# Attention mix on one core: the clamp pass writes the first exponential slice itself, and part of the last fold moves ahead of the last B unit

## The chip, the core and the metric

The kernel runs on one core of one Trainium2 chip. The metric is device microseconds of one execution.

Names of the engines: PE is the matrix engine (PEld its weight loads), VectorE is "DVE" in the profile, ScalarE is "ACT", GpSimd is "POOL", SP issues most DMAs.

## The reference

Two attention blocks on the same input, gated per token:

```python
def reference(A_x, A_wqkv, A_wo, B_x, B_wqkv, B_wo, gate_w):
    x = A_x                                   # [1, 2048, 640]
    g = _sigmoid((x * gate_w).sum(-1, keepdims=True))
    a = _A_ref(x, A_wqkv, A_wo)               # 32 heads of 20, full softmax attention over 2048 keys
    b = _B_ref(x, B_wqkv, B_wo)               # 32 heads, each query sees 8 keys, 2 apart
    return g * a + (1 - g) * b
```

## The kernel before

Everything is in bf16 with fp32 sums. Block A is cut into 2048 "units": one head, 128 keys, 512 queries. Each unit needs a score matmul, 512 exponentials per partition, and a value matmul. Block B is cut into eight token units of 256 tokens; each has projections, eight product passes on VectorE, a small softmax, eight more product passes, and a summation on PE. The whole of B's work, the projections of A, and the output folds are "side work": they run in gaps.

The instruction order is made at build time by a scheduler written in the kernel file. It keeps its own estimate of each engine's clock and decides tile by tile.

**A tile and its third bank.** PSUM is used in full: two score buffers of three banks each, one bank for the value sums (`obank`), one side bank. (The Trainium skill, "PSUM — Partial Sum Buffer", section "Specifications (TRN2)", gives eight banks of 512 fp32 values per partition; 3 + 3 + 1 + 1 is eight.) A tile of scores always fills the first two banks of a score buffer, and ScalarE turns them into exponentials with one instruction. The third bank has three possible users: a third unit for ScalarE, a unit for VectorE (a "ride"), or side work.

```python
BANKS = [(sbank, 0), (score[0], 1024), (score[1], 1024)]   # side bank, third bank of each score buffer
...
def next_tile():
    x = 1 + s % 2
    free = not bank_used[x] and bank_free[x] <= now + XTOL and not crowded(x)
    n = 3 if free else 2
    ...
        if len(us) == 2 and not ride:
            ride = wanted(...)                 # give the third bank to VectorE?
            if ride:
                break
        us.append(...)                         # else a unit for ScalarE
```

**Rides.** VectorE makes exponentials from integers: a number written as the bit pattern of a bf16 is a power of two with a straight line between, and four shifted copies ("slices"), weighted and summed by the value matmul, smooth that line. Four rides of one key block make a "quad".

```python
def wanted(js):
    idle = max(now, exps[s - 2].end + LAT["act"]) + 0.4 - sch.avail["dve"]
    if idle < -DWAIT:
        return None
    if not dopen:                              # a new quad would have to be opened
        if ulock[len(dquads) % 2] or len(dquads) > cur["pv"] + 1 or now < D0 or not (
                idle >= DIDLE2 or idle >= DIDLE and done.get(...) and
                bdone[0] >= (now - BT0) / (BT1 - BT0) * BALL):
            return None                        # at most two quads open; B must be on schedule
    ...
# clamp pass, one per ride, from PSUM:
uD[d % 2][:, 512 * i:512 * (i + 1)], side[x], UOFF, 0.0, op0=ALU.add, op1=ALU.max
# slice passes, four per quad, 2048 elements:
for k in range(K):
    eD[:, sl % NS, 0:512 * n].bitcast(I16), uD[d % 2][:, 0:512 * n], 0.25, SHIFTS[k], op0=ALU.mult, op1=ALU.add
```

**Side work and third banks.** Side work normally has only the side bank. It may take third banks as well when block B is behind a straight-line schedule:

```python
XPRIO, XLATE, XT0, XT1 = 2.5, 6.6, 150.0, 880.0
def xprio():                                   # priority up to which side work may take third banks
    return XPRIO if bdone[0] >= (sch.avail["pe"] - XT0) / (XT1 - XT0) * BALL else XLATE
```

B's priority is 6, so it passes only when it is late. `bdone` sums the VectorE time that B has had; `BALL` is its total.

**The last fold.** For the last 512 tokens, partial output sums (`gen_prefold`) are made ahead of the last head group, once B is done and the other head groups are normalised.

Of the kernel before, what the change touches and what calls it, by code (L numbers as in the profile page):

```python
# [5 lines left out]
FP32 = mybir.dt.float32  # L6
# [8 lines left out]
P = 128  # L15
# [28 lines left out]
LN2 = 0.6931471805599453  # L44
STEP = 512.0
OCT = STEP * SCALE / LN2
TOP = 96
UOFF = 31 * STEP
SHIFTS = (12024.625, 12055.875, 12088.375, 12120.125)
WEIGHTS = (1.0, 0.83984375, 0.71484375, 0.59375)  # L50
K = len(SHIFTS)

# [208 lines left out]
def _build(ctx, nc, A_x, A_wqkv, A_wo, B_wqkv, B_wo, gate_w, out):  # L261
# [29 lines left out]
    ND = 2  # L291
    dst = [sb([P, 512], BF16, "dst%d" % i) for i in range(ND)]
    qbnd = sb([P, 512], BF16, "qbnd")
# [6 lines left out]

    uD = [sb([P, 4 * 512], U16, "uD%d" % i) for i in range(2)]
    gtr = uD[1][:, 0:1024].bitcast(FP32)
# [5 lines left out]
    gwT = sb([P, CN], BF16, "gwT")  # L308
    qabs = [sb([P, 512], BF16, "qabs%d" % i) for i in range(2)]
    kmx4 = sb([P, 4], FP32, "kmx4")  # L310
# [389 lines left out]
    def gen_d(d):  # L700

        n = len(ridden[d])
        while d > 0 and not done.get(("dq", d - 1)):
            yield ("cond",)
        g, kb = dquads[d]
        q = GROUPS[g][1]
        while cur["pv"] < d - 1 or not done.get(("v", kb, q // 4)):
            yield ("cond",)
        for k in range(1, K):
            T("pool", 0.3, lambda e, k=k: e.tensor_scalar(  # L710
                vS[:, d % 2, k - 1, :], _ap(vA, (kb * NQ + q) * 4 * DV, [[1, 4 * DV]]), WEIGHTS[k], None, op0=ALU.mult),
              reads=[("vA", kb, q // 4), "vAones"], writes=[("vS", d % 2, k)])
        for k in range(K):
            sl = sbase[d] + k
            while npv[0] <= sl - NS:
                yield ("cond",)
            yield ("dve", DAHEAD, sch.free(("eD", sl % NS)))
            T("dve", 0.11 + 0.1334 * n, lambda e, k=k, sl=sl: e.tensor_scalar(  # L718
                eD[:, sl % NS, 0:512 * n].bitcast(I16), uD[d % 2][:, 0:512 * n], 0.25, SHIFTS[k], op0=ALU.mult, op1=ALU.add),
              reads=[("uD", d % 2, i) for i in range(n)], writes=[("eD", sl % NS)])  # L720
            done[("ds", d, k)] = True
        ulock[d % 2] = False
        done[("dq", d)] = True

# [157 lines left out]

    pre = lambda i: stage[:, i * 1024:(i + 1) * 1024].bitcast(FP32)
    tail_bank = {}
# [9 lines left out]
    def gen_prefold():  # L894
        while not (done.get(("b", 2 * QCN - 1)) and all(done.get(("norm", POS[QCN - 1, q])) for q in range(1, NQ))):
            yield ("cond",)
        rd = [("oTd", (QCN - 1) % 2, q) for q in range(1, NQ)] + ["woA_d", "woBp"] + [
            ("oB", hu, f0) for hu in range(2) for f0 in range(0, CN, 2)]
        qs = None
        for i in range(3):  # L900
            b = yield from bank()
            if i < 2:
                yield from mm_group(b, fold_mms(side[b][:, :], 2 + i, qs, 0, 512, True), rd, mmc(512))
            else:
                for blk in range(4):
                    yield from mm_group(b, fold_mms(side[b][:, blk * P:(blk + 1) * P], blk, qs, 512, D, True), rd, mmc(128), per=3)
            yield ("dve",)
            t = T("dve", dvc(512), lambda e, b=b, i=i: e.tensor_copy(pre(i), side[b][:, :]), reads=[("side", b)],
                  writes=[("pre", i)] + [("prod", w) for w in range(5)])
            release(b, t)  # L910
        done["prefold1"] = True
# [10 lines left out]
    def gen_prefold2():  # L922
# [4 lines left out]
        qs = None  # L927
        for blk in range(2):
            b = yield from bank()
            yield from mm_group(b, fold_mms(side[b][:, :], blk, qs, 0, 512, True), rd, mmc(512), last=False)  # L930
            tail_bank[blk] = b
        done["prefold"] = True

    def tail():
# [15 lines left out]
        mm(("score", 1), [fold_mms(b3[:, blk * P:(blk + 1) * P], blk, q, 512, D, False)[0] for blk in range(4)], False)  # L950
        for blk in range(2):
            b = tail_bank[blk]
            mm(("side", b), fold_mms(side[b][:, :], blk, q, 0, 512, False), True)
        for blk in (2, 3):
            mm(("score", 0), fold_mms(score[0][:, (blk - 2) * 512:(blk - 1) * 512], blk, q, 0, 512, False), False)
        T("dve", dvc(512), lambda e: e.tensor_tensor(
            _ap(stage, 3 * 1024 + 512, [[D, 4], [1, P]]), _ap(b3, 0, [[P, 4], [1, P]]),
            stage[:, 2048:3072].bitcast(FP32).rearrange("p (b c) -> p b c", c=P), ALU.add),
          reads=[("score", 1), ("pre", 2)], writes=["tout_r"])
        for blk in range(2):  # L960
            b = tail_bank[blk]
            T("act", actc(512), lambda e, b=b, blk=blk: e.activation(tcol(blk, 0, 512), side[b][:, :], ACTF.Copy),
              reads=[("side", b)], writes=[("tout", blk)])
        for blk in (2, 3):
            T("dve", dvc(512), lambda e, blk=blk: e.tensor_tensor(
                tcol(blk, 0, 512), score[0][:, (blk - 2) * 512:(blk - 1) * 512], pre(blk - 2), ALU.add),
              reads=[("score", 0), ("pre", blk - 2)], writes=[("tout", blk)])
        for blk in range(4):
# [82 lines left out]
    XT0 = 150.0  # L1051
    XT1 = 880.0

# [191 lines left out]
    BT0 = 230.0  # L1245
    BT1 = 900.0
    BALL = 186.0
# [62 lines left out]
    def d_close():  # L1310
# [4 lines left out]
        if ridden[d]:  # L1315
            nsl[0] += K
            add_gen(gen_d(d), DLOW + 0.0001 * d)
        else:
            ulock[d % 2] = False
            done[("dq", d)] = True  # L1320
# [45 lines left out]
    def qk(s):  # L1366
# [22 lines left out]
        if rides[s]:  # L1389

            run_dve(t.end + LAT["pe"] - RFILL)
            t = T("dve", 0.69, lambda e: e.tensor_scalar(  # L1392
                uD[d % 2][:, 512 * i:512 * (i + 1)], side[x], UOFF, 0.0, op0=ALU.add, op1=ALU.max),
              reads=[("side", x)], writes=[("uD", d % 2, i)])
# [4 lines left out]
    def exp(s):  # L1399
# [5 lines left out]
        if n == 3:  # L1405
            bank_free[x] = exps[s].end + LAT["act"]

    def pv(units, slices):

# [9 lines left out]
        for d, k in slices:  # L1419
            g, kb = dquads[d]  # L1420
            sl = (sbase[d] + k) % NS
            rd.add(("eD", sl))
            if k:
                rd.add(("vS", d % 2, k))
            for i, j in enumerate(ridden[d]):
                v = vS[:, d % 2, k - 1, j * DV:(j + 1) * DV] if k else vA[:, kb, GROUPS[g][1], j, :]
                lst.append((g, kb, j, v, eD[:, sl, 512 * i:512 * (i + 1)]))
            left_d[g] -= len(ridden[d])
            npv[0] += 1
        for g, kb, j, _, _ in lst:  # L1430
# [68 lines left out]
    def pv_slot(s, force=False):  # L1499
# [10 lines left out]
        while not first and cur["pv"] < len(dquads) and dquads[cur["pv"]][0] == pvg and len(slices) < NS:  # L1510
# [9 lines left out]
            if not ok:  # L1520
                urge(d, DHIGH)
                run_until(("ds", d, k), DHIGH)
            elif not end_g and sch.ready(("eD", (sbase[d] + k) % NS)) > sch.avail["pe"]:
                break
# [9 lines left out]
    def slices_ready():  # L1534
# [4 lines left out]
        n = 0  # L1539
        while n < NS and k + n < K and done.get(("ds", d, k + n)) and sch.ready(  # L1540
                ("eD", (sbase[d] + k + n) % NS)) <= sch.avail["pe"]:
            n += 1
# [86 lines left out]
```

## Time and profile before

| | before |
|---|---|
| time, median of three runs | 881.18 us (879.49 to 881.99); with a fourth run, used from "The result" on, 880.38 us |
| units on ScalarE / rides on VectorE | 1768 / 280 |
| exponential instructions | 754: 260 of three units, 494 of two (280 with a ride, 214 without) |
| last exponential ends | 865.7 us of a span of 879.1 us |

The next line is the first part of the page: busy us of each engine, share of the span, instruction count.

```profile
PE 852.9 (97%) x13406; PEld 312.7 (36%) x13406; DVE 701.7 (80%) x1192; ACT 834.9 (95%) x788; POOL 226.7 (26%) x309
```

The groups by shape: line, engine, operation, out<-in, shapes, count | busy us, mean ns of one | idle time of the engine just before, and what ended it.

```profile
L1402 ACT ACTIVATE ebuf<-score 128x1024 bf16<-128x1024 f32 x494 | 475.4, 1037 | 15.2 <-PE score L1379 13.5 <-ACT ebuf L1402 0.2
L1402 ACT ACTIVATE ebuf<-score 128x1536 bf16<-128x1536 f32 x260 | 364.3, 1471 | 7.0 <-PE score L1379 5.9 <-ACT ebuf L1402 0.3
...
L718 DVE TENSOR_SCALAR eD<-uD 128x2048 int16<-128x2048 uint16 x280 | 190.5, 705 | 14.1 <-PE obank L1441 13.5
L1392 DVE TENSOR_SCALAR uD<-score 128x512 uint16<-128x512 f32 x280 | 187.7, 683 | 43.5 <-PE score L1379 41.6
...
L487 PE MATMUL side<-xT,kvw 128*32 128x256 bf16 x1920 | 76.3, 275 | 2.1 <-DVE qkvB L769 1.6 <-DVE oB L876 0.2 <-DVE qbnd L614 0.2
...
L487 PE MATMUL score<-xT,kvw 128*32 128x256 bf16 x480 | 19.6, 274 | 0.0
```

ScalarE's exponentials fill the run. A ride costs VectorE a clamp of 0.68 us and a quarter of four slice passes. And B's projections (the 128x256 matmuls on `xT,kvw`, 2400 in all) run to one fifth in third banks: out is `score` for 480 of them.

The end of the run, as a timeline (start us, us, engine and line, what, count, idle before):

```profile
846.29 0.42 DVE L876 SCALAR_TENSOR_TENSOR oB<-side,rB 128x256 bf16<-128x256 f32 x1 [0.52 <-PE side L487]
...
852.79 0.61 PE L487 MATMUL score<-woBp,oB 128*32 128x512 bf16 x8 [0.32 <-DMA oTd<-oN]
...
861.61 4.13 ACT L1402 ACTIVATE ebuf<-score 128x1536 bf16<-128x1536 f32 x3
874.23 0.60 ACT L962 ACTIVATE stage<-side 128x512 bf16<-128x512 f32 x1 [8.48 <-PE side L943]
```

The last exponential ends at 861.61 + 4.13 = 865.74 us, and 13.4 us of tail follow. The first leftover fold had waited for a DMA that brings normalised rows, not for B: the last B unit ends with the last write of `oB`, its output, at 846.7 us, 19 us before the last exponential ends.

A caution on PE: its 97% includes filler matmuls that keep it busy (1832 of 13406). The Trainium skill, "Perfetto Trace Analysis", section "Identifying the Most-Contended Engine", warns that matmul busy time does not say well how close PE is to its peak.

### The profile page before, as it was taken

What the parts mean: (1) busy time and instruction counts of PE and PEld (TensorE: products, weight loads), DVE (VectorE), ACT (ScalarE), POOL (GpSimd) and SP (SyncE); (2) the same over time, 40 slices, a digit from 0 to 9 for tenths busy, and PEclk for the clock granted to TensorE, in tenths of its full rate; (3) what the DMA queues carried; (4) which work ended last, traced back from release to release, by engine and by line L of the source; (5) the groups of instructions that cost most, each with busy time, mean ns of one, the idle gap of its engine ahead of it and who ended that gap; (6) DMA issues with size and microseconds to landing.
All of it is one profiled execution on the core that took longest, in us unless ns stands there. A gap on an engine that the chain in (4) does not pass through costs nothing.

```text
span 879.1 us, 31181 instructions
## 1 busy us (share of the span) xinstructions
PE 852.9 (97%) x13406; PEld 312.7 (36%) x13406; DVE 701.7 (80%) x1192; ACT 834.9 (95%) x788; POOL 226.7 (26%) x309
## 2 busy tenths in 40 slices
PE   8999999999989999999999999999999999999997
PEld 4333333434333333433333333333343334333223
DVE  6567778888788776988888997887887788989864
ACT  5999999999989999999999999999999999999994
POOL 5031027411331212152322133221023312312320
PEclk9999999999999999999999999999999999999999
DMA  9112112001010101010000100010010000100000
GB/s 292 33 39 45 43 31 71 17 15 29 23 28 23 41 21 25 13 28 20 21 18 17 34 20 20 27 28 14 13 36 20 21 19 27 27 12 12 24 6 32
DMA packets 40893, 28.19 MB, mean 32 GB/s; under 512 B 23732, under 2 KB 39556, under 8 KB 40756
## 3 DMA queue, kind: packets, MB, share of 16 engines
q1 hardware_dynamic: 40756, 26.20, 11.4%
q8 instruction: 106, 1.74, 0.8%
q14 instruction: 31, 0.25, 0.1%
HBM read 11.94 MB, written 2.62 MB: 17 GB/s over the span
## 4 chain that ended last, share of the span: by engine, by line
PE 78%; ACT 10%; DVE 6%; POOL 3%; issue 3%; DMA 0%; SPq 0%; DVEq 0%; ACTq 0%; POOLq 0%
PE score L1379 23%; PE obank L1441 18%; PE side L487 16%; ACT ebuf L1402 9%; PE score L487 8%; PE obank L1462 4%; PE score L1462 3%; PE side L1462 2%; POOL vS L710 1%; DVE eD L718 1%; PE side L798 1%; POOL kvw L732 1%; DVE stage L785 1%; POOL oN L690 1%; DVE oTt L679 0%
## 5 line engine op out<-in xcount | busy, mean ns | idle before, releaser
L1402 ACT ACTIVATE ebuf<-score 128x1024 bf16<-128x1024 f32 (+1 forms) x754 | 819.3, 1186 | 22.2 <-PE score L1379 19.5
L1379 PE MATMUL score<-qT,kT 32*128 32x512 bf16 x2048 | 298.4, 384 | 10.6 <-ACT ebuf L1402 7.5
L1392 DVE TENSOR_SCALAR uD<-score 128x512 uint16<-128x512 f32 x280 | 187.7, 683 | 43.5 <-PE score L1379 41.6
L718 DVE TENSOR_SCALAR eD<-uD 128x2048 int16<-128x2048 uint16 x280 | 190.5, 705 | 14.1 <-PE obank L1441 13.5
L710 POOL TENSOR_SCALAR vS<-vA 128x84 bf16<-128x84 bf16 x210 | 145.7, 697 | 128.3 <-PE obank L1441 118.4
L1379 PEld LDWEIGHTS score<-qT,kT 32*128 32x128 bf16 x2048 | 73.8, 91 | 269.8 <-issue 127.4
L1441 PE MATMUL obank<-ebuf,vA 128*21 128x512 bf16 x1768 | 164.0, 385 | 3.6 <-ACT ebuf L1402 1.2
L685 POOL TENSOR_TENSOR rcp<-rcp,gA 128x16 f32<-128x16 f32 x31 | 12.4, 400 | 463.1 <-DVE rcp L683 463.1
L487 PE MATMUL side<-xT,kvw 128*32 128x256 bf16 (+1 forms) x2030 | 85.6, 281 | 2.1 <-DVE qkvB L769 1.6
L1441 PE MATMUL obank<-eD,vS 128*21 128x512 bf16 x840 | 73.7, 381 | 0.0
L1441 PEld LDWEIGHTS obank<-ebuf,vA 128*21 128x21 bf16 x1768 | 40.3, 89 | 86.5 <-issue 70.7
L1462 PE MATMUL obank<-xT,zero 128*32 128x512 bf16 x808 | 66.8, 384 | 0.0
L1462 PE MATMUL score<-xT,ident 128*32 128x512 bf16 x708 | 59.2, 382 | 0.0
L487 PEld LDWEIGHTS side<-xT,kvw 128*32 128x32 bf16 x2030 | 48.0, 96 | 30.8 <-issue 16.1
L785 DVE TENSOR_TENSOR stage<-qkvB 128x1280 bf16<-128x1280 bf16 x64 | 52.9, 856 | 0.1
L861 DVE TENSOR_TENSOR stage<-qkvB,repB 128x1280 bf16<-128x1280 bf16 x64 | 50.7, 816 | 0.6 <-DMA repB<-eB 0.5
L487 PE MATMUL side<-stage,ident 128*32 128x512 bf16 (+1 forms) x704 | 44.9, 348 | 0.0
L487 PE MATMUL score<-xT,kvw 128*32 128x256 bf16 (+2 forms) x730 | 41.8, 311 | 0.0
L769 DVE CAST qkvB<-side 128x512 bf16<-128x512 f32 (+1 forms) x57 | 33.9, 595 | 7.2 <-PE side L487 7.0
L690 POOL TENSOR_TENSOR oN<-oTt,rcp 128x512 bf16<-128x512 f32 x31 | 35.1, 1131 | 2.4
L679 DVE STREAM_TRANSPOSE oTt<-obank 128x512 f32<-128x512 f32 x32 | 22.8, 713 | 9.7 <-PE obank L1441 9.1
L692 DVE STREAM_TRANSPOSE oN<-oN 128x512 bf16<-128x512 bf16 x32 | 22.4, 700 | 6.7 <-POOL oN L690 6.5
(165 smaller groups left out, 674.0 us busy)
## 6 DMA issues: line engine op xcount, KB each, us to landing
repB<-eB SPq DMA_DIRECT2D x128, 32.0 KB
WqP<-in_A_wqkv_dram SPq DMA_DIRECT2D x16, 160.0 KB
stage<-in_B_wqkv_dram SPq DMA_DIRECT2D x1, 2400.0 KB
oTd<-oN SPq DMA_DIRECT2D x108, 20.0 KB
qT<-dst SPq DMA_DIRECT2D x104, 20.0 KB
out_dram<-outsb SPq DMA_DIRECT2D x12, 160.0 KB
kvw<-in_A_wqkv_dram SPq DMA_DIRECT2D x2, 800.0 KB
oTd<-in_A_x_dram SPq DMA_DIRECT2D x2, 640.0 KB
```

Of the source, the lines that this page charges most:

```text
L487: ins = e.matmul(o[j:k, :], l[:, j:k], r, start=(first and i == 0), stop=(last and i == n - 1), skip_group_check=True)
L690: T(en, c2, lambda e: e.tensor_tensor(oo, ii, ib, ALU.mult), reads=["rcp", "oTt"], writes=["oN0"])
L710: T("pool", 0.3, lambda e, k=k: e.tensor_scalar(vS[:, d % 2, k - 1, :], _ap(vA, (kb * NQ + q) * 4 * DV, [[1, 4 * DV]]), WEIGHTS[k], None, ...
L718: T("dve", 0.11 + 0.1334 * n, lambda e, k=k, sl=sl: e.tensor_scalar(eD[:, sl % NS, 0:512 * n].bitcast(I16), uD[d % 2][:, 0:512 * n], 0.25, ...
L769: t = TB(dvc(n * TOK), lambda e, o=o, i=i: e.tensor_copy(o, i), reads=[("side", b)], writes=[key])
L785: TB(dvc(CN * TOK, 2), lambda e, w=w, ks=ks: e.tensor_tensor(prodB(w), qB[:, :, :], ks, ALU.mult), reads=["qB", "kB"], writes=[("prod", w) ...
L861: TB(dvc(CN * TOK, 2), lambda e, w=w, vs=vs, rr=rr: e.tensor_tensor(prodB(w), vs, rr, ALU.mult), reads=["vB", ("repB", w4 % 2)], writes=[( ...
L1379: ins = e.matmul(o, kT[32 * j:32 * j + 32, q, kb * P:(kb + 1) * P], qT[g % NQT][32 * j:32 * j + 32, :], start=True, stop=True)
L1392: t = T("dve", 0.69, lambda e: e.tensor_scalar(uD[d % 2][:, 512 * i:512 * (i + 1)], side[x], UOFF, 0.0, op0=ALU.add, op1=ALU.max), reads=[ ...
L1402: exps[s] = T("act", actc(512 * n), lambda e: e.activation(ebuf[s % NE][:, 0:512 * n], score[s % 2][:, 0:512 * n], ACTF.Exp, scale=LN2 / S ...
L1441: ins = e.matmul(obank[32 * j:32 * j + DV, :], v, src, start=(kb == 0), stop=(last and k >= len(lst) - 4), skip_group_check=True)
L1462: ins = e.matmul(o[32 * j:32 * j + 32, :], w[:, 32 * j:32 * j + 32] if best else w[:, :], xT[:, 0, 0:512], start=bool(best), stop=bool(bes ...
```

## The change

The intent: choose the integer step so that the clamp pass already writes the bit pattern of a bf16, that is, slice 0. Three integer additions make the other slices. VectorE saves one slice pass in four. The scheduler's constants are retuned, and the leftover folds of the first two token blocks need only the second-last B unit, so they can go ahead of the last one.

```diff
-STEP = 512.0
+STEP = 128.0
-UOFF = 31 * STEP
-SHIFTS = (12024.625, 12055.875, 12088.375, 12120.125)
-WEIGHTS = (1.0, 0.83984375, 0.71484375, 0.59375)
+SHIFTS = (0, 32, 64, 96)
+WEIGHTS = (1.0, 0.83984375, 0.70703125, 0.59375)
+UOFF = 15992.765
...
-            T("pool", 0.3, lambda e, k=k: e.tensor_scalar(
+            T("pool", 0.7, lambda e, k=k: e.tensor_scalar(
...
-        for k in range(K):
-            sl = sbase[d] + k
+        for k in range(1, K):
+            sl = sbase[d] + k - 1
...
-                eD[:, sl % NS, 0:512 * n].bitcast(I16), uD[d % 2][:, 0:512 * n], 0.25, SHIFTS[k], op0=ALU.mult, op1=ALU.add),
+                eD[:, sl % NS, 0:512 * n].bitcast(I16), uD[d % 2][:, 0:512 * n].bitcast(I16), SHIFTS[k], None, op0=ALU.add),
...
+        done[("dq", d)] = True
+        while not done.get(("p0", d)):
+            yield ("cond",)
         ulock[d % 2] = False
-        done[("dq", d)] = True
...
-        while not (done.get(("b", 2 * QCN - 1)) and all(...)):
+        while not (done.get(("b", 2 * QCN - 2)) and all(...) and done.get(("q", NG - 1))):
...
-    XT1 = 880.0
+    XT1 = 860.0
-    BT1 = 900.0
+    BT1 = 880.0
...
-                uD[d % 2][:, 512 * i:512 * (i + 1)], side[x], UOFF, 0.0, op0=ALU.add, op1=ALU.max),
+                uD[d % 2][:, 512 * i:512 * (i + 1)].bitcast(I16), side[x], UOFF, 0.0, op0=ALU.add, op1=ALU.max),
...
+                src = eD[:, sl, 512 * i:512 * (i + 1)] if k else uD[d % 2][:, 512 * i:512 * (i + 1)]
```

(The wait for `p0` holds the u-buffer until the value matmul has used slice 0. Cut: the places where partial sums are stored, the order of blocks in the tail, bookkeeping of slices. The 0.3 and 0.7 are only what the scheduler assumes for a GpSimd instruction; the instruction is the same.)

More of the change, by code (lines that the diff above doesn't have):

```diff
@@ L291, in _build @@
     ND = 2
-    dst = [sb([P, 512], BF16, "dst%d" % i) for i in range(ND)]
+    dst2 = sb([P, ND * 512], BF16, "dst")
+    dst = [dst2[:, i * 512:(i + 1) * 512] for i in range(ND)]
     qbnd = sb([P, 512], BF16, "qbnd")
@@ L299, in _build @@
     gA = [sb([P, 16], FP32, "gA%d" % i) for i in range(2)]
-    uD = [sb([P, 4 * 512], U16, "uD%d" % i) for i in range(2)]
+    uD = [sb([P, 4 * 512], BF16, "uD%d" % i) for i in range(2)]
     gtr = uD[1][:, 0:1024].bitcast(FP32)
@@ L308, in _build @@
     gwT = sb([P, CN], BF16, "gwT")
-    qabs = [sb([P, 512], BF16, "qabs%d" % i) for i in range(2)]
+    qabs2 = sb([P, 2 * 512], BF16, "qabs")
+    qabs = [qabs2[:, i * 512:(i + 1) * 512] for i in range(2)]
     kmx4 = sb([P, 4], FP32, "kmx4")
@@ L879, in gen_b @@
         done[("b", u)] = True
-    pre = lambda i: stage[:, i * 1024:(i + 1) * 1024].bitcast(FP32)
+    pre = lambda i: (dst2[:, 0:1024], qabs2[:, :], stage[:, 2048:3072])[i].bitcast(FP32)
     tail_bank = {}
@@ L894, in gen_prefold @@
     def gen_prefold():
-        while not (done.get(("b", 2 * QCN - 1)) and all(done.get(("norm", POS[QCN - 1, q])) for q in range(1, NQ))):
+        while not (done.get(("b", 2 * QCN - 2)) and all(done.get(("norm", POS[QCN - 1, q])) for q in range(1, NQ))
+                   and done.get(("q", NG - 1))):
             yield ("cond",)
-        rd = [("oTd", (QCN - 1) % 2, q) for q in range(1, NQ)] + ["woA_d", "woBp"] + [
-            ("oB", hu, f0) for hu in range(2) for f0 in range(0, CN, 2)]
         qs = None
         for i in range(3):
+            while i == 2 and not done.get(("b", 2 * QCN - 1)):
+                yield ("cond",)
+            rd = [("oTd", (QCN - 1) % 2, q) for q in range(1, NQ)] + ["woA_d", "woBp"] + [
+                ("oB", hu, f0) for hu in range(1 + (i == 2)) for f0 in range(0, CN, 2)]
             b = yield from bank()
             if i < 2:
-                yield from mm_group(b, fold_mms(side[b][:, :], 2 + i, qs, 0, 512, True), rd, mmc(512))
+                yield from mm_group(b, fold_mms(side[b][:, :], i, qs, 0, 512, True), rd, mmc(512))
             else:
@@ L908, in gen_prefold @@
             t = T("dve", dvc(512), lambda e, b=b, i=i: e.tensor_copy(pre(i), side[b][:, :]), reads=[("side", b)],
-                  writes=[("pre", i)] + [("prod", w) for w in range(5)])
+                  writes=[("pre", i)] + [[("dst", 0), ("dst", 1)], [("qabs", 0), ("qabs", 1)], [("prod", w) for w in range(5)]][i])
             release(b, t)
@@ L927, in gen_prefold2 @@
         qs = None
-        for blk in range(2):
+        for blk in (2, 3):
             b = yield from bank()
@@ L950, in tail @@
         mm(("score", 1), [fold_mms(b3[:, blk * P:(blk + 1) * P], blk, q, 512, D, False)[0] for blk in range(4)], False)
-        for blk in range(2):
+        for blk in (2, 3):
             b = tail_bank[blk]
             mm(("side", b), fold_mms(side[b][:, :], blk, q, 0, 512, False), True)
-        for blk in (2, 3):
-            mm(("score", 0), fold_mms(score[0][:, (blk - 2) * 512:(blk - 1) * 512], blk, q, 0, 512, False), False)
+        for blk in range(2):
+            mm(("score", 0), fold_mms(score[0][:, blk * 512:(blk + 1) * 512], blk, q, 0, 512, False), False)
         T("dve", dvc(512), lambda e: e.tensor_tensor(
@@ L959, in tail @@
           reads=[("score", 1), ("pre", 2)], writes=["tout_r"])
-        for blk in range(2):
+        for blk in (2, 3):
             b = tail_bank[blk]
@@ L963, in tail @@
               reads=[("side", b)], writes=[("tout", blk)])
-        for blk in (2, 3):
+        for blk in range(2):
             T("dve", dvc(512), lambda e, blk=blk: e.tensor_tensor(
-                tcol(blk, 0, 512), score[0][:, (blk - 2) * 512:(blk - 1) * 512], pre(blk - 2), ALU.add),
-              reads=[("score", 0), ("pre", blk - 2)], writes=[("tout", blk)])
+                tcol(blk, 0, 512), score[0][:, blk * 512:(blk + 1) * 512], pre(blk), ALU.add),
+              reads=[("score", 0), ("pre", blk)], writes=[("tout", blk)])
         for blk in range(4):
@@ L1315, in d_close @@
         if ridden[d]:
-            nsl[0] += K
+            nsl[0] += K - 1
+            done[("ds", d, 0)] = True
             add_gen(gen_d(d), DLOW + 0.0001 * d)
@@ L1406, in exp, with slice_keys @@
             bank_free[x] = exps[s].end + LAT["act"]
+    def slice_keys(d, k):
+        return [("eD", (sbase[d] + k - 1) % NS)] if k else [("uD", d % 2, i) for i in range(len(ridden[d]))]
     def pv(units, slices):
@@ L1420, in pv @@
             g, kb = dquads[d]
-            sl = (sbase[d] + k) % NS
-            rd.add(("eD", sl))
+            rd.update(slice_keys(d, k))
+            sl = (sbase[d] + k - 1) % NS
             if k:
                 rd.add(("vS", d % 2, k))
+                npv[0] += 1
+            else:
+                done[("p0", d)] = True
             for i, j in enumerate(ridden[d]):
                 v = vS[:, d % 2, k - 1, j * DV:(j + 1) * DV] if k else vA[:, kb, GROUPS[g][1], j, :]
-                lst.append((g, kb, j, v, eD[:, sl, 512 * i:512 * (i + 1)]))
+                src = eD[:, sl, 512 * i:512 * (i + 1)] if k else uD[d % 2][:, 512 * i:512 * (i + 1)]
+                lst.append((g, kb, j, v, src))
             left_d[g] -= len(ridden[d])
-            npv[0] += 1
         for g, kb, j, _, _ in lst:
@@ L1522, in pv_slot @@
                 run_until(("ds", d, k), DHIGH)
-            elif not end_g and sch.ready(("eD", (sbase[d] + k) % NS)) > sch.avail["pe"]:
+            elif not end_g and sch.ready(*slice_keys(d, k)) > sch.avail["pe"]:
                 break
@@ L1539, in slices_ready @@
         n = 0
-        while n < NS and k + n < K and done.get(("ds", d, k + n)) and sch.ready(
-                ("eD", (sbase[d] + k + n) % NS)) <= sch.avail["pe"]:
+        while n < NS and k + n < K and closed[d] and ridden[d] and done.get(("ds", d, k + n)) and sch.ready(
+                *slice_keys(d, k + n)) <= sch.avail["pe"]:
             n += 1
```

## The prediction

> **What bounds the kernel now.** ScalarE. The table of busy shares gives ScalarE 834.9 us of 879.1 (95%), of which 819.3 us are the 754 exponentials (costliest groups). In every 40 us stretch from 40 to 840 us it is busy 37.1 to 39.9 us; the rest is start (first exponential at 21.2 us) and tail (last one ends near 865.8 us). PE shows 97%, but 1832 of its matmuls (the groups of the filler line) are filler; in fours at about 0.22 us a set they are some 100 us (estimate), so PE has slack. VectorE shows 80%.
>
> Of 2048 score units (128x512), VectorE takes 280 ("rides", 70 quads of four), ScalarE 1768. By form, a two-unit exponential takes 1.037 us and a three-unit one 1.471 us, so a unit moved off ScalarE is worth about 0.43 us there. The schedule, made at build time, lets units ride as it sees room on VectorE; so the time follows VectorE's cost per ride.
>
> **What the change removes.** Before, a quad costs four clamp passes from PSUM (0.683 us each) and four slice passes of 2048 elements (0.705 us mean, 0.684 median). After, the clamp output is itself slice 0, and three integer adds follow. So one slice pass in four goes: 70 x 0.60 to 0.70 us = 42 to 49 us of VectorE at today's number of rides (in the timeline, passes in a row start 0.60 us apart).
>
> The remaining passes should keep their duration. The Trainium skill, "VectorE: DVE Perf Modes", section "The perf-mode tier table", puts one-source 16-bit SBUF-to-SBUF operations in the 4x mode; today's pass at 0.62 to 0.68 us for 2048 elements fits, and the add is again one-source. The clamp still reads fp32 from PSUM: 0.68 us.
>
> VectorE's 13.5 us of waits before slices, for the matmul that frees a slice buffer, should shrink.
>
> **Added or moved.** Each additional ride puts four instead of one value matmuls on PE: three sets shared by four units, about 0.16 us per ride (estimate), taken from filler. The u-buffer is held longer, but at most two quads were open already, so this costs nothing.
>
> **On the critical path.** None of the freed VectorE time directly; it pays through more rides. With VectorE's share held at 80%, a ride costing 1.05 to 1.2 us instead of 1.2 to 1.39, and each ride shortening VectorE's own budget, rides rise to about 310 to 325: 30 to 45 x 0.43 to 0.44 us = 13 to 19 us. Estimate 16 us.
>
> **Tail.** After the last exponential come 13 us: three leftover folds on PE (2.38, 2.38 and 2.69 us), final products, output. But today the first fold starts (852.8 us) on the landing of the last normalised rows (852.65), not on the last B unit, which ended at 846.7. So letting folds go ahead of B gains little by itself: 1 to 2 us.
>
> **Prediction:** 863 us, range 853 to 873. Faster by over 2%: 0.52; within 2%: 0.45; slower: 0.03.
>
> **Shown right** by: slice passes three per quad, each near 0.68 us; 305 to 330 clamp passes; ScalarE exponentials down to about 800 to 806 us at an unchanged 95% share; fewer filler matmuls; VectorE share 77 to 82%. **Shown wrong** by: rides still near 280 with VectorE's share falling (then open quads or PSUM banks limit, not VectorE), integer adds much slower than 0.7 us, or new ScalarE waits on PE.
>
> **What would spoil it:** changed pacing constants delay B and lengthen the tail, or ride slots (one per tile), not VectorE, limit rides. Better if VectorE's share rises.

## The result

The changed kernel takes 874.42 us (median; 873.98 to 875.19), the kernel before 880.38 us in the same rounds. The ratio is 0.9931, with a 95% interval of 0.9913 to 0.995. Ratios here and below are the mean time of one kernel's fast runs over that of the other's of the same rounds, so not quite the ratio of the medians quoted. The gain is real and small: 6 us where 16 to 18 were expected, and outside the stated range.

The profile after, the same views: engines, groups by shape, end of the run.

```profile
PE 852.7 (98%) x13106; PEld 308.0 (35%) x13106; DVE 680.7 (78%) x1157; ACT 831.0 (95%) x819; POOL 221.1 (25%) x324
```

```profile
L1410 ACT ACTIVATE ebuf<-score 128x1024 bf16<-128x1024 f32 x607 | 581.6, 1035 | 16.1 <-PE score L1387 12.6 <-ACT ebuf L1410 0.3
...
L1410 ACT ACTIVATE ebuf<-score 128x1536 bf16<-128x1536 f32 x178 | 251.1, 1476 | 4.7 <-PE score L1387 4.5
L1400 DVE TENSOR_SCALAR uD<-score 128x512 int16<-128x512 f32 x300 | 201.9, 684 | 59.4 <-PE score L1387 57.2 <-ACT g L671 0.5
...
L720 DVE TENSOR_SCALAR eD<-uD 128x2048 int16<-128x2048 int16 x225 | 154.7, 712 | 7.6 <-PE obank L1455 7.0
...
L489 PE MATMUL side<-xT,kvw 128*32 128x256 bf16 x1380 | 57.4, 276 | 0.4 <-DVE qkvB L773 0.2
...
L489 PE MATMUL score<-xT,kvw 128*32 128x256 bf16 x1020 | 41.8, 274 | 0.0
```

```profile
841.89 0.42 DVE L880 SCALAR_TENSOR_TENSOR oB<-side,rB 128x256 bf16<-128x256 f32 x1 [0.28 <-PE side L489]
...
846.35 0.40 PE L489 MATMUL score<-woBp,oB 128*32 128x512 bf16 x4
...
856.74 3.77 ACT L1410 ACTIVATE ebuf<-score 128x1536 bf16<-128x1536 f32 x3 [0.24 <-PE score L1387]
867.19 0.60 ACT L969 ACTIVATE stage<-side 128x512 bf16<-128x512 f32 x1 [6.68 <-PE side L950]
```

What is to be seen:

- The arithmetic did what it should. 225 slice passes for 75 quads, 712 ns each (705 before). The clamp still takes 0.68 us.
- Only 20 more rides (280 to 300). VectorE is 21 us *less* busy than before: the freed time was not spent.
- The number of exponential instructions rose from 754 to 785. Of the 607 two-unit ones, 300 carry a ride, so 307 had no use of their third bank; before it was 494 - 280 = 214.
- B's projections now run to 1020 of 2400 in third banks, against 480.
- The last B unit ends at 842.3 us, 18 us before the last exponential (19 us in the kernel before). In neither kernel of the pair does B end last.

There is bookkeeping that ties these together. Every tile has two units in its first banks; so 2 x (exponentials) + (third banks used for a unit) = 2048 units, up to a last partial tile; for instance 2 x 785 + 300 + 178. More third banks lost to side work means more exponential instructions. What they cost can be read from the 14 profiles: a least-squares fit of the exponentials' total busy time gives 0.416 us per unit and 0.111 us per instruction, with no run further off than 1.7 us. (The Trainium skill, "ScalarE: Activation LUTs", section "What ACT_TABLE_LOAD costs", gives 186 ns plus 0.833 ns per element for an instruction with immediate scale and bias (constants inside the instruction), which makes 1.04 us for 1024 elements (an estimate from the page), and an overlap of about 93 ns between instructions; the trace has a mean of 1.037 us for one instruction.) So the 20 rides are worth -8.3 us, and the 31 more instructions +3.5 us. Measured, the exponentials fell from 819.3 to 815.6 us. The last one ends 5.2 us earlier (860.5 us), and the tail shrank by 1.0 us (13.4 to 12.4), which is within its scatter (see e7).

### The profile page after: what moved, and what is told of

Read it like the earlier page. It is cut to its first block, busy times and chain, and to the rows that moved or that the text cites. A ratio compares the mean times of both kernels' runs of the same rounds, so it can differ in the third digit from the quotient of the medians.

```text
span 872.9 us, 30620 instructions
## 1 busy us (share of the span) xinstructions
PE 852.7 (98%) x13106; PEld 308.0 (35%) x13106; DVE 680.7 (78%) x1157; ACT 831.0 (95%) x819; POOL 221.1 (25%) x324
## 4 chain that ended last, share of the span: by engine, by line
PE 73%; ACT 17%; DVE 6%; issue 4%; DMA 0%; POOL 0%; SPq 0%; DVEq 0%; ACTq 0%
PE score L1387 23%; PE obank L1455 17%; ACT ebuf L1410 16%; PE side L489 14%; PE score L489 9%; PE obank L1476 3%; PE score L1476 2%; PE side L1476 1%; DVE uD L1400 1%; DVE eD L720 1%; DVE stage L789 1%; DVE qkvB L773 1%; PE side L802 1%; PE score L609 1%; DVE stage L865 0%
## 5 line engine op out<-in xcount | busy, mean ns | idle before, releaser
L1410 ACT ACTIVATE ebuf<-score 128x1024 bf16<-128x1024 f32 (+1 forms) x785 | 815.6, 1135 | 20.8 <-PE score L1387 17.1
L1387 PE MATMUL score<-qT,kT 32*128 32x512 bf16 x2048 | 315.0, 385 | 11.0 <-ACT ebuf L1410 4.9
L1400 DVE TENSOR_SCALAR uD<-score 128x512 int16<-128x512 f32 x300 | 201.9, 684 | 59.4 <-PE score L1387 57.2
L720 DVE TENSOR_SCALAR eD<-uD 128x2048 int16<-128x2048 int16 x225 | 154.7, 712 | 7.6 <-PE obank L1455 7.0
L489 PE MATMUL side<-xT,kvw 128*32 128x256 bf16 (+1 forms) x1540 | 70.5, 287 | 0.4 <-DVE qkvB L773 0.2
L489 PE MATMUL score<-xT,kvw 128*32 128x256 bf16 (+1 forms) x1220 | 60.4, 292 | 0.0
L1476 PE MATMUL obank<-xT,zero 128*32 128x512 bf16 x680 | 55.7, 384 | 0.0
L489 PEld LDWEIGHTS side<-xT,kvw 128*32 128x32 bf16 x1540 | 36.9, 96 | 24.4 <-issue 15.0
L1476 PE MATMUL score<-xT,ident 128*32 128x512 bf16 x424 | 36.7, 381 | 0.0
L489 PEld LDWEIGHTS score<-xT,kvw 128*32 128x32 bf16 x1220 | 28.6, 96 | 22.3 <-issue 15.2
L1455 PE MATMUL obank<-uD,vA 128*21 128x512 bf16 x300 | 29.2, 379 | 0.0
```

What stands on the lines that cost most here:

```text
L489: ins = e.matmul(o[j:k, :], l[:, j:k], r, start=(first and i == 0), stop=(last and i == n - 1), skip_group_check=True)
L720: T("dve", 0.11 + 0.1334 * n, lambda e, k=k, sl=sl: e.tensor_scalar(eD[:, sl % NS, 0:512 * n].bitcast(I16), uD[d % 2][:, 0:512 * n].bitcas ...
L1387: ins = e.matmul(o, kT[32 * j:32 * j + 32, q, kb * P:(kb + 1) * P], qT[g % NQT][32 * j:32 * j + 32, :], start=True, stop=True)
L1400: t = T("dve", 0.69, lambda e: e.tensor_scalar(uD[d % 2][:, 512 * i:512 * (i + 1)].bitcast(I16), side[x], UOFF, 0.0, op0=ALU.add, op1=ALU. ...
L1410: exps[s] = T("act", actc(512 * n), lambda e: e.activation(ebuf[s % NE][:, 0:512 * n], score[s % 2][:, 0:512 * n], ACTF.Exp, scale=LN2 / S ...
L1455: ins = e.matmul(obank[32 * j:32 * j + DV, :], v, src, start=(kb == 0), stop=(last and k >= len(lst) - 4), skip_group_check=True)
```

## The experiments

Theory V is the prediction's: VectorE's room alone sets the number of rides, and rides set the time. The rival, theory S: rides, third units and B's side work compete for third banks, and B must be finished too, so the time is set by two chains. Later runs split off theory Q: the rule of at most two open quads limits the rides, not VectorE.

All kernels gave correct results unless said. "Tail" is the span minus the end of the last exponential in the profiled run; "B ends" is the end of the last write of `oB` in that run. The scheduler prints nothing to the chip, but its decisions can be counted when the program is built; "planned" numbers in the expectations are such counts, and estimates of times in them rest partly on the order in which that planner's own clock puts the kernels.

| run | time us (median) | ratio to before | rides | exponentials | last one ends | tail | B ends |
|---|---|---|---|---|---|---|---|
| before | 880.38 | 1 | 280 | 754 | 865.7 | 13.4 | 846.7 |
| changed | 874.42 | 0.9931 | 300 | 785 | 860.5 | 12.4 | 842.3 |
| e1_twice | 892.54 | 1.0148 | 287 | 802 | 872.0 | 19.6 | 877.3 |
| e2_cap70 | 880.01 | 1.0003 | 280 | 785 | 869.2 | 9.8 | 833.4 |
| e3_core | 896.31 | 1.019 | 308 | 778 | 854.5 | 39.5 | 875.6 |
| e4_half | 879.89 | 1.0002 | 320 | 797 | 858.8 | 19.3 | 863.7 |
| e5_tuned_after | 868.92 | 0.988 | 296 | 726 | 855.7 | 11.2 | 834.4 |
| e6_tuned_before | 872.34 | 0.9919 | 280 | 730 | 858.4 | 12.0 | 834.1 |
| e7_latefold | 874.64 | 0.9947 | 300 | 785 | 858.1 | 13.8 | 841.1 |
| e8_before_pool | 888.67 | 1.0107 | 280 | 782 | 863.3 | 23.3 | 868.2 |
| e9_open3 | 890.25 | 1.0124 | 328 | 735 | 847.2 | 41.9 | 874.8 |
| e10_tuned_half | 871.40 | 0.9905 | 312 | 729 | 858.3 | 11.7 | 827.2 |
| e11_tuned_twice | 883.73 | 1.0049 | 288 | 724 | 862.6 | 18.8 | 867.1 |
| e12_open3_light | 865.93 | 0.9846 | 316 | 727 | 851.2 | 13.4 | 836.4 |

The last two columns belong together. In the six runs where B ends after the last exponential (e1, e3, e4, e8, e9, e11) the tail is 18.8 to 41.9 us; in the other eight it is 9.8 to 13.8 us.

### e1_twice: give the saved pass back

```diff
             done[("ds", d, k)] = True          # in the loop over slices of the changed kernel
+            (before it, for k == K - 1: the same integer add once more, into the same slice)
```

> The changed kernel with its third integer add run twice, so VectorE gets the removed pass back (four slice passes a quad) and nothing else differs. Theory V (the prediction's: VectorE's room alone sets the number of rides, and each ride is worth 0.43 us): rides fall from 300 back to about 280, time rises by about 20 x 0.43 = 9 us, to 883 us, with about as many exponentials as the changed kernel plus none. Theory S (a ride, a third ScalarE unit and the side work of unit B all compete for the third PSUM bank of a tile, so a slower VectorE also delays unit B, which then takes third banks): the built schedule has 287 rides and 802 exponentials; time about 889 us, 14 to 15 us over the changed kernel and so more than the rides are worth.

Measured: 892.54 us, 287 rides, 802 exponentials. Against the changed kernel's profile the span grew by 18.7 us. The exponentials took 7.6 us of that (823.2 against 815.6 us busy) and the tail 7.2 us, because B ended later (877.3 against 842.3 us); most of the rest, 3.6 us, is longer idle time of ScalarE between exponentials. At these constants the pass is worth far more than its rides, which is what theory S says and theory V does not. It is also slower than the kernel before, although VectorE now has the same number of passes per quad: the constants of the changed kernel suit only the changed kernel.

### e2_cap70: the same 280 rides as before

```diff
             t_end = sch.avail["act"]
+            if len(dquads) >= 70:
+                return None                    # placed ahead of this line
```

> The changed kernel, but no quad is opened after the 70th, so it has the 280 rides of the kernel before; VectorE's freed time stays free. Theory V: the whole gain came through the rides, so it is gone: about 880 us, as before. Theory S: the first 70 quads run as in the changed kernel, 20 units go back to ScalarE late in the run (785 exponentials planned): about 879 to 880 us, last exponential 7 us later than in the changed kernel (some 868 us). Both agree on the time; what the run shows is the price of a ride on the chip, expected 0.25 to 0.43 us. If it were near 875 us, rides would have no worth and the gain came from elsewhere (the tail).

Measured: 880.01 us, ratio 1.0003 to before. The last exponential ends 8.7 us later than in the changed kernel, 0.43 us per ride given up, and the tail is 2.6 us shorter. The price of a ride that the prediction used was right; it was the number of rides that was not. VectorE is at 75% in this run, so its room does not help as long as no ride spends it. (The equal time is a balance, though: against the kernel before, the last exponential ends 3.4 us later, with 31 more exponential instructions, and the tail is 3.6 us shorter.)

### e3_core: the arithmetic alone, without the new constants and the early fold

```diff
-    XT1 = 860.0        BT1 = 880.0        T("pool", 0.7, ...
+    XT1 = 880.0        BT1 = 900.0        T("pool", 0.3, ...
-        while not (done.get(("b", 2 * QCN - 2)) and ...
+        while not (done.get(("b", 2 * QCN - 1)) and ...
```

> Only the arithmetic part: the clamp writes slice 0 and three integer adds follow; the pacing constants, the cost that the scheduler assumes for the GpSimd scaling and the early fold are as in the kernel before. Theory V: the rides (308 in the built schedule) are all that counts: 28 x 0.43 = 12 us under the kernel before, 868 to 870 us. Theory S: the exponentials end some 9 us earlier than in the kernel before (about 855 to 857 us), but unit B is not done by then and the tail after the last exponential grows from 13 to over 30 us; time about 895 to 899 us, slower than before.

Measured: 896.31 us, 1.9% slower than before, with 28 more rides. The end of the run (timeline):

```profile
852.95 1.55 ACT L1410 ACTIVATE ebuf<-score 128x1024 bf16<-128x1024 f32 x2
853.15 13.05 SPq L854 DMA_DIRECT2D repB<-eB  x16
...
867.52 1.56 DVE L865 TENSOR_TENSOR stage<-qkvB,repB 128x1280 bf16<-128x1280 bf16 x2 [0.97 <-DMA repB<-eB]
869.14 3.40 PE L489 MATMUL side<-stage,ident 128*32 128x512 bf16 x32 [13.98 <-DVE stage L865]
...
875.20 0.42 DVE L880 SCALAR_TENSOR_TENSOR oB<-side,rB 128x256 bf16<-128x256 f32 x1 [0.18 <-PE side L489]
...
888.28 0.60 ACT L969 ACTIVATE stage<-side 128x512 bf16<-128x512 f32 x1 [33.50 <-PE side L950]
```

The exponentials end 11 us earlier than before, as theory V has it, but the last B unit is still at its softmax weights (the DMAs of `repB`) and product passes, and ScalarE stands idle for 33.5 us. Unit B is the second chain, and in this run it is the one that ends last.

### e4_half: free VectorE further

```diff
-                eD[:, sl % NS, 0:512 * n].bitcast(I16), uD[d % 2][:, 0:512 * n].bitcast(I16), SHIFTS[k], ...
+                eD[:, sl % NS, 0:256 * n].bitcast(I16), uD[d % 2][:, 0:256 * n].bitcast(I16), SHIFTS[k], ...
```

(The scheduler's cost is halved too; the value matmuls read the written half. The values are wrong, yet the result passed the comparison.)

> Wrong result on purpose: the three slice passes of the changed kernel cover half the elements, so VectorE is relieved by another 1 us or so per quad; the value matmuls read the written half. Theory V: rides rise by another 35 to 45 and time falls by another 15 us, to about 860 us. Theory S: rides rise (320 in the built schedule) but they hold third banks, so unit B falls behind and 343 exponentials instead of 307 are two-unit ones without a ride; time about 882 us, no better than the changed kernel.

```profile
L1410 ACT ACTIVATE ebuf<-score 128x1024 bf16<-128x1024 f32 x663 | 633.9, 1035 | 21.5 <-PE score L1387 17.9
...
L1400 DVE TENSOR_SCALAR uD<-score 128x512 int16<-128x512 f32 x320 | 217.3, 686 | 98.0 <-PE score L1387 94.3
L1410 ACT ACTIVATE ebuf<-score 128x1536 bf16<-128x1536 f32 x134 | 190.8, 1467 | 3.9 <-PE score L1387 3.7
...
L720 DVE TENSOR_SCALAR eD<-uD 128x1024 int16<-128x1024 int16 x240 | 103.6, 463 | 8.4 <-PE obank L1455 7.4
```

The end of B in this run, from VectorE's timeline:

```profile
862.73 1.01 DVE L880 SCALAR_TENSOR_TENSOR oB<-score,rB 128x512 bf16<-128x512 f32 x2
```

Measured: 879.89 us. The slice passes fell by 51 us in total (154.7 to 103.6 us busy), rides rose by 20, and the run is 0.7% slower than the changed kernel (ratio to before 1.0002 against 0.9931). 663 - 320 = 343 exponentials have no use of their third bank, and VectorE waits 94.3 us for PE's scores before its clamps, up from 57.2 us. The exponentials still ended 1.7 us earlier than in the changed kernel; what was lost is the tail, 6.9 us longer, for B ended at 863.7 us, after them. This is the clearest count against theory V: cheaper passes did bring rides, but VectorE's share fell to 73% and the time did not follow.

### e5_tuned_after and e6_tuned_before: the same care for both kernels

If the constants matter this much, then before and changed should be compared with constants chosen alike. For each kernel I let the scheduler plan many random sets of its pacing constants (500; both had as many candidates), and took the best-planned one. No arithmetic differs.

```diff
 e5, from the changed kernel:  DAHEAD 0.5 -> 0.4, XT0 150 -> 160, XT1 860 -> 940, DTIME 12 -> 13,
                               BT0 230 -> 215, BT1 880 -> 900, DWAIT 1.0 -> 1.3
 e6, from the kernel before:   DAHEAD 0.5 -> 0.4, XT0 150 -> 170, XT1 880 -> 870, DTIME 12 -> 13,
                               BT0 230 -> 215, BT1 900 -> 840, D0 50 -> 54, "pool" 0.3 -> 0.7
```

> The changed kernel with other pacing constants (later side-work goal, slices issued with less patience), chosen because the built schedule has few exponentials: 296 rides, 727 exponentials of which only 130 are two-unit without a ride (300, 785 and 307 in the changed kernel). Theory V: four rides fewer than the changed kernel, so about 876 us. Theory S: third banks are no longer given away, so fewer exponentials and the last one ends 4 to 5 us earlier: 867 to 871 us.

> The kernel before with pacing constants chosen in the same way from as many candidates: 280 rides as before, but 730 exponentials instead of 755. Theory V: same rides, same time: 880 us. Theory S: 25 exponentials fewer and less waiting of unit B: 873 to 877 us; that is as good as the changed kernel without any change to the arithmetic, and 5 to 8 us behind the changed kernel tuned alike, so the arithmetic is worth some 6 us, not 16, wherever both are tuned.

The groups of e5, then of e6:

```profile
L489 PE MATMUL side<-xT,kvw 128*32 128x256 bf16 x2400 | 94.2, 274 | 4.9 <-DVE qkvB L773 4.1 <-DVE qbnd L616 0.7
...
L1410 ACT ACTIVATE ebuf<-score 128x1536 bf16<-128x1536 f32 x300 | 419.1, 1465 | 8.5 <-PE score L1387 7.1
L1410 ACT ACTIVATE ebuf<-score 128x1024 bf16<-128x1024 f32 x426 | 410.4, 1037 | 12.1 <-PE score L1387 10.0
```

```profile
L1402 ACT ACTIVATE ebuf<-score 128x1536 bf16<-128x1536 f32 x308 | 430.6, 1476 | 8.3 <-PE score L1379 7.3
L1402 ACT ACTIVATE ebuf<-score 128x1024 bf16<-128x1024 f32 x422 | 407.0, 1040 | 8.8 <-PE score L1379 6.5 <-ACT ebuf L1402 0.2
...
L487 PE MATMUL side<-xT,kvw 128*32 128x256 bf16 x2360 | 91.6, 274 | 2.0 <-DVE qkvB L769 1.4
...
L487 PE MATMUL score<-xT,kvw 128*32 128x256 bf16 x40 | 1.8, 275 | 0.0
```

Measured: 868.92 us and 872.34 us. In both, B's projections run almost wholly in the side bank, and B is still done in time. So with these constants B does not need the third banks that it took in the first two kernels. Three things follow. The kernel before, with other constants and no new arithmetic, is at least as fast as the changed kernel (872.34 against 874.42 us, from different rounds; e7, in the same rounds as e6, took 874.64 us). The changed kernel with four rides *fewer* and 59 exponentials fewer is 0.5% faster (0.988 against 0.9931). And between the two tuned kernels, run in the same rounds, 3.4 us are left: 16 rides more take 5.5 us off the exponentials (811.3 against 816.8 us busy), of which the last exponential's end keeps 2.8 us. The size of e6's gain was larger than expected, so the change's own part came out smaller. Fewer exponential instructions explain e5's gain over the changed kernel (4.3 us of busy time, of 4.9 us by which the last one ends earlier), but e6's gain over the kernel before only in part: there it is 2.5 us of 7.3 us, and most of the rest is shorter idle time of ScalarE before exponentials (17.1 against 22.2 us).

### e7_latefold: the early fold undone

```diff
-        while not (done.get(("b", 2 * QCN - 2)) and ...
+        while not (done.get(("b", 2 * QCN - 1)) and ...
```

> The changed kernel with the early fold undone: the first leftover folds wait for the last B unit again. If the fold matters, the tail after the last exponential grows by 2 us or more, to 877 us. If it does not because those folds wait anyway for the landing of the last normalised rows (both theories): 874 to 875 us, as the changed kernel.

Measured: 874.64 us against 874.42. The early fold brings nothing in this schedule, and the trace says why: in the changed kernel B ends at 842.3 us, and the first leftover fold starts only at 846.35 us, so nothing was held back by the last B unit. (The profiled tails are 13.8 us here and 12.4 us in the changed kernel, with the same numbers of rides and exponentials; so 1 us between two profiled tails is not clear of scatter. In runs where B ends late, e4 for one, the first folds do start before B's end; whether the early fold pays there was not tested.)

### e8_before_pool: a number that does no work

```diff
-            T("pool", 0.3, lambda e, k=k: e.tensor_scalar(
+            T("pool", 0.7, lambda e, k=k: e.tensor_scalar(
```

> The kernel before, with one number changed: the scheduler assumes 0.7 us instead of 0.3 us for the GpSimd scaling of the value rows. No instruction changes its work; only the order does. Rides stay at 280. Theory V: same rides and same VectorE, so 879 to 881 us. Theory S: the schedule gives side work more third banks (298 two-unit exponentials without a ride instead of 214, 782 exponentials instead of 755) and time rises by 8 to 12 us, to about 890 us, although no engine has more real work per ride.

Measured: 888.67 us, 1.1% slower than before with the same instructions per ride and the same 280 rides; 782 exponentials, and 980 of the 2400 projection matmuls in third banks. Yet the last exponential ends 2.5 us earlier than before; the loss is in the tail (23.3 against 13.4 us), for B ends at 868.2 us, after it. The number is closer to the profile's mean of this instruction before (0.697 us; its median is 0.421 us, and spans on GpSimd are rough in this profile), and the schedule it leads to is worse. A single schedule scatters by more than the change under study is worth.

### e9_open3: allow a third open quad

```diff
-        if ulock[len(dquads) % 2] or len(dquads) > cur["pv"] + 1 or ...
+        if ulock[len(dquads) % 2] or len(dquads) > cur["pv"] + 2 or ...
```

(From e5, as are e10 and e11; e12 starts from this run.)

> The tuned changed kernel (296 rides, 868.9 us), with three quads allowed open instead of two; no pass gets cheaper. Theory V (VectorE's room limits the rides): rides stay near 296 and so does the time, 867 to 871 us. Theory Q (the rule of two open quads limits the rides, and unit B, which must end as well, limits the time): the built schedule has 328 rides and the last exponential ends some 10 us earlier, near 845 to 848 us, but unit B is not finished then: the tail after the last exponential grows from 11 us to 35 us or more, and the time is 885 to 892 us.

```profile
L1400 DVE TENSOR_SCALAR uD<-score 128x512 int16<-128x512 f32 x328 | 220.2, 686 | 40.5 <-PE score L1387 37.5
```

The end of the same run, as a timeline:

```profile
843.87 3.36 ACT L1410 ACTIVATE ebuf<-score 128x1024 bf16<-128x1024 f32 x3
...
854.65 10.60 SPq L854 DMA_DIRECT2D repB<-eB  x16
...
868.19 3.54 PE L489 MATMUL score<-stage,ident 128*32 128x512 bf16 x32 [11.63 <-DVE stage L865]
...
874.38 0.43 DVE L880 SCALAR_TENSOR_TENSOR oB<-score,rB 128x256 bf16<-128x256 f32 x1 [0.18 <-PE score L489]
...
883.41 0.60 ACT L969 ACTIVATE stage<-side 128x512 bf16<-128x512 f32 x1 [27.42 <-PE side L950]
```

Measured: 890.25 us, 328 rides, last exponential at 847.2 us, tail 41.9 us. With no pass made cheaper there are 32 rides more than in e5; so with e5's constants VectorE had the room, and a bookkeeping rule held the rides back. (This does not carry over to the changed kernel's own constants, for which no such run was made. A count of the plan at build time gives 304 rides there with the same edit, against 300; the same count gives e9's 328.) And the exponentials ended 8.4 us earlier while the run became 2.4% longer (ratio 1.0124 against 0.988), some 21 us, because the last B unit still had its softmax, products and sums to do.

### e10_tuned_half and e11_tuned_twice: VectorE's time at the tuned constants

The edits are those of e4 and e1, on e5.

> Wrong values on purpose: the tuned changed kernel with slice passes of half the elements, some 0.7 us of VectorE less per quad (462 ns instead of 712 ns a pass in the earlier half-pass run). Theory V: 20 to 30 rides more, 8 to 12 us less, near 858 us. Theory Q: 312 rides in the built schedule, but no gain, 869 to 875 us.

> The tuned changed kernel with the third add pass run twice, so VectorE gets the removed pass back. Theory V: back to about 280 rides, +16 x 0.414 = 7 us: 875 to 877 us. Theory Q: 288 rides in the built schedule and nearly the same number of exponentials (725), but unit B ends later too: 880 to 886 us, with a tail over 15 us. If it were near 872.3 us (the tuned kernel before), the pass alone would be the whole difference between the two tuned kernels.

Measured: 871.40 us with 312 rides, and 883.73 us with 288 rides. With half passes the exponentials take 6.7 us less than in e5 (804.6 against 811.3 us busy), but ScalarE's idle time before them rises from 20.5 to 29.8 us, and the last one ends 2.7 us *later*. The next line is e10's; in e5's counterpart above, ScalarE's wait for PE's scores is 7.1 us in place of 13.7.

```profile
L1410 ACT ACTIVATE ebuf<-score 128x1536 bf16<-128x1536 f32 x279 | 392.8, 1474 | 14.5 <-PE score L1387 13.7
```

With the doubled pass, rides fall by only 8 and the exponentials grow by 1.7 us, but the last one ends 6.9 us later (3.9 us of that is more idle time before exponentials) and the tail grows by 7.7 us, with B's end at 867.1 against 834.4 us. VectorE's time thus acts through waits and B's end, hardly through rides, when it becomes scarce, and brings no gain when it becomes plentiful. (The one-sidedness is what two schedules show; e8 is a warning not to read 3 us out of one of them.)

### e12_open3_light: take B out of the way

```diff
                             xT[:, c, t0:t0 + TOK]) for c in range(CN)]      # B's projections, in e9
+                            xT[:, c, t0:t0 + TOK]) for c in range(2)]
```

(Wrong result.)

> Wrong result on purpose: the three-open-quads kernel, with unit B's projections lightened (two of the five contraction chunks instead of five; VectorE's passes of unit B all stay). Theory V: rides and time do not depend on unit B's matmuls: the same as the three-quads kernel within 2 us. Theory Q: with unit B out of the way the ridden units pay: 316 rides, the last exponential near 850 us and a short tail, 862 to 867 us, that is 20 us or more under the three-quads kernel, although VectorE has the same work per ride and per B unit.

```profile
L489 PE MATMUL side<-xT,kvw 128*32 128x256 bf16 x960 | 41.0, 274 | 1.8 <-DVE qkvB L773 1.8
```

Measured: 865.93 us; last exponential at 851.2 us, tail 13.4 us. Against e9 the run is 24 us shorter though the exponentials end 4 us later. VectorE's passes for B are all still there; what was lightened is PE's work and the time that it holds banks. So B's matmuls and their banks help to hold its end back. By how much is not shown: e12 also has 12 rides fewer than e9, some 15 us of VectorE's passes (an estimate: 12 clamps of 0.69 us and 9 slice passes of 0.71 us), and B ends 38 us earlier (836.4 against 874.8 us).

## Why the prediction was wrong

- **"What bounds the kernel now: ScalarE."** Half right. ScalarE's exponentials bound most of the run, but unit B's chain has to end as well. In the pair itself it ends 19 and 18 us before the last exponential, so it does not set the time there directly; the scheduler guards it there by giving it third banks, and these cost exponential instructions. e3 and e9 lay the second limit bare, with tails of 39.5 and 41.9 us.
- **The costs.** Right. One slice pass in four went; the others stayed near 0.7 us. The Trainium skill, "VectorE: DVE Perf Modes", section "The perf-mode tier table", lists 693 ns for 2048 elements in bf16; the int16 add has a median of 685 ns here. (The prediction says "16-bit" and names this table, which has bf16 alone; that the condition is 16-bit tensors, whatever their type, stands in the same page's section "What auto-detection actually checks".) The waits before slices fell from 13.5 to 7.0 us. Filler matmuls fell from 1832 to 1472. A ride is worth 0.43 us of ScalarE (e2).
- **"So the time follows VectorE's cost per ride" and "with VectorE's share held at 80% ... rides rise to about 310 to 325".** This is the step that failed. Rides rose by 20, not 30 to 45, and VectorE's share was not held: it fell to 78%, its busy time by 21 us. Cheaper passes bring some rides, but most of the freed time is not spent, and the time does not follow: halved slice passes gave 320 rides at a share of 73% and a run 0.7% slower (e4), and no gain at e5's constants (e10). There the rule of two open quads held the rides: with a third quad allowed there were 328 at full pass cost (e9), and even these did not shorten the run. The prediction had named that rule, and concluded that it "costs nothing". What held the rides at 300 under the changed kernel's own constants stays open. The missing 10 to 25 rides are 4 to 10 us at 0.416 us.
- **What the sum left out.** Side work took more third banks: 31 more exponential instructions, +3.5 us by the fit. The causes are mixed: with the old constants and the new arithmetic B's projections already take 820 of 2400 there, against 480 (e3), the change tightens B's schedule on top (XT1, BT1; 1020), and one assumed duration alone gives 980 without one more ride (e8). In e4 there were 343 exponentials without a use of the third bank, and B's late end ate the gain.
- **The tail.** 1 to 2 us expected, 1.0 us found, but this is less than the tail's scatter, and not the early fold's doing: the time is the same without it (e7).
- **"Changed pacing constants"** were named as a risk to the tail. They were more than that: a constant that does no work moves the time by 1.1% (e8), and the arithmetic alone, without its constants and the early fold, loses 1.9% (e3).

What is shown: that the time does not follow VectorE's cost per ride (e4, e10), B's end as the second limit (e3, e9, e12 and the table's last columns), the rule of two open quads as what limits rides at e5's constants (e9), and fewer lost third banks as the gain of e5 (for e6 only in part). What stays open: what holds the rides in the changed kernel itself; whether B's matmuls hold it back by PE time or by the time they keep banks, since e12 lightens both, and how much of e12's gain comes from its 12 rides fewer; what the change is worth on average over schedules, for which there are only the pair as given (6.0 us) and the pair tuned alike (3.4 us); and which of the seven constants of e5 matter.

The fastest kernel with a correct result is e5, the changed arithmetic with other constants: 868.92 us, ratio 0.988 to before. It beats both kernels.

## What to carry to other kernels

Time freed on an engine that is not the bottleneck pays only through a decision that spends it; before counting on it, read the rule that makes that decision, and loosen it alone as a test. A second chain that is kept in time does not show as a bottleneck in a profile; shorten the first on purpose and look at what is left running at the end, and read off in each run where each chain ends. With a build-time scheduler, retune both kernels alike before crediting a change with the difference, and change a number that does no work to learn how far schedules scatter.

## What the Trainium skill lacked or had wrong

- "VectorE: DVE Perf Modes", section "The perf-mode tier table", has times for bf16 and fp32 only, and none for a 16-bit integer. Here a one-source int16 add from SBUF to SBUF took a median of 685 ns for 2048 elements (e4: 421 ns for 1024), close to the table's 693 ns for bf16.
- "ScalarE: Activation LUTs" states its cost formula under a section on table loads ("What ACT_TABLE_LOAD costs"), where one does not look for it. It holds: 1.037 us for 1024 elements, and over 14 profiles 0.416 us per 512 elements plus 0.111 us per instruction, against 0.427 us and 93 ns net of overlap (estimates worked out from the page).
- "Perfetto Trace Analysis", section "Identifying the Most-Contended Engine", says to optimise the engine with the highest occupancy first. Here ScalarE at 95% was relieved by 13.3 us of exponentials (e9 against e5) and the run became 21 us longer, because another chain had to end too. The page has no test for a second chain that must also end.
- No page read gives a measured duration for so short a GpSimd instruction beside a busy VectorE: scaling 84 elements took a median of 418 ns, a mean of 638 ns and at most 3.7 us in the changed kernel (spans on GpSimd are rough in this profile). "SBUF — State Buffer", section "SBUF: two separate sides", describes a port lock between the two engines that would fit; no run here tested it.
